# Moving the second weights, the state loads and four layer-2 steps in the opening of a fused attention and Fourier-mixing kernel

## The chip, the cores and the metric

One NeuronCore of one Trainium2 chip runs the whole program. The metric is device time in microseconds (us), the median of several executions. TensorE is written PE in the profile, VectorE DVE, ScalarE ACT, GpSimd POOL, SyncE SP. SyncE does no arithmetic here: it only issues DMAs, one after the other.

## What is computed

There are 8 batches. `x` has the shape (8 batches, 8 heads, 512 rows, 64), `state` (8, 8, 32, 64). The first part is a cross attention of x and state in both directions, per head:

```python
scores  = x @ state.T / 8 ; xread = softmax(scores) @ state      # 512 rows
scores2 = state @ x.T / 8 ; sread = softmax(scores2) @ x         #  32 rows
x = concat([xread, sread], rows)     # (8, 544, 512) after the heads are put side by side
```

The second part works on each batch's 544 x 512 matrix:

```python
mixed = real(fft(fft(x, axis=rows), axis=columns))
u  = x + mixed
un = (u - mean(u)) / sqrt(var(u) + 1e-6)          # over the 512 columns
out = u + relu(un @ w_ch1) @ w_ch2                # 512 -> 2048 -> 512
```

The real part of the two transforms is written as products with cosine and sine tables, after folding rows and columns that the tables treat alike.

## The kernel before

**Order.** The order of the work on every engine is written out by hand (a manual schedule): instructions stand on their engine in the order in which the source calls them, and each engine works strictly through its own list. What is issued behind a waiting instruction on the same engine waits with it. Batch 0 and the table set-up are the opening. Then comes one long hand-written stretch, in which batch 0's layer 1, batch 1's attention and both axes of batch 1's transform are interleaved. From there on a function `weave` mixes streams of steps for `b = 1..7` by fractions of a stage: layer 2 of batch b-1, layer 1 of batch b, the reads and the transform of batch b+1, the scores of batch b+2 and the load of x of batch b+3. A stream `(steps, lo, hi)` spreads its steps evenly between the fractions `lo` and `hi`.

**Names.**
- `load_x(b)` issues seven DMAs on SyncE (L145), which bring x of batch b into an f32 tile `xs` in packets of 256 bytes. Two `xs` tiles take turns. `cast_x` (L148) or, for batch 2, `cast_columns` (L1118) casts it on POOL into the bf16 tile `xin`.
- `turned[b]()` issues the DMA transposes on SyncE: two of the state blocks into `sT` (L377) and four of `xin` into `xT` (L388). `turned[2, 0]` is the two state transposes of batch 2 alone. `scores(i)` (PE, `esp`, L437) needs them, its results go through the exponential on ACT (L442), and `turn_scores(g)` (PE, `eTp`, L449) turns these.
- `turn_in_dram(lo, hi)` (L155) copies the states of batches lo to hi-1 from DRAM to DRAM with the 32 rows of each head in reverse order; `load_state(lo, hi, s_dram)` (L113) loads the turned states into an f32 tile; `state_blocks` (L168) writes them, as bf16, into the block-diagonal tile `stb`, four copies on POOL. The states of batches 0 to 2 lie in one tile, those of batches 3 to 7 in another.
- `first_weights(lo, hi)` and `second_weights(lo, hi)` (L310, L325) load quarters of `w_ch1` and `w_ch2` with a cast from f32 to bf16, 512 KB on the chip's side each. Their DMAs are issued by POOL, on a queue of their own.
- `gate` copies are tiny POOL instructions that read one column of a tile. Each holds POOL's list until the tile has been written: L1132 waits for w1's last quarter, L1167 for batch 2's x, L1169 for batch 1's second fold, L1172 for the last quarter of w2. The last four columns of batch 2's x are cast behind L1172, and so the transposes of batch 2's x wait for w2.
- Batch 1's reads are `r1[0]` to `r1[7]`. `r1[0]` reads the low rows and copies them on POOL (L519), `r1[1]` and `r1[2]` fold them on POOL (L523 to L531, `XEl`, `XQl`). The full rows are folded on VectorE (L534 to L549, `XQ`).
- `L[0..15]` are layer 1's steps of batch 0: 16 matmuls of 128 columns (L936) into a PSUM tile `ph`, then a Relu on ACT (L938). `M[4*i + q]` is layer 2's step of row tile i and quarter q of w2: 4 matmuls of 512 columns (L990) into the PSUM tile `po` of row tile i, which is held from q = 0 until the result is formed (`ot`, VectorE, L957) after q = 3. `ph` and `po` share three PSUM buffers (`psF`).
- `over_s1(j)` (`gp`, L783) is batch 1's transform over the rows, `over_d1(k)` (`yp`, L679 and L680) that over the columns; `add1`, `centre1` and `turn_u1` (L684, L840, L851) add, subtract the mean and turn the result for layer 1.
- `stats_of` computes mean and variance into a tile `mv` (VectorE, L339); a `root` turns it into `rstd` with two POOL instructions (L343, L344). The roots of batches 0 and 1 are collected and called late, in a block. `mv` has six buffers.
- A finished tile whose rows go out in reverse is stored to `r_dram` (L971) and from there, once that has landed, to the output (L972). Others go out directly (L961).

Of the kernel before, what the change touches and what calls it, by code (L numbers as in the profile page):

```python
# [12 lines left out]
F32 = mybir.dt.float32  # L13
# [17 lines left out]
def kernel(  # L31
# [8 lines left out]
    nc = tc.nc  # L40
    B, H, S, D = x.shape
# [11 lines left out]
    s_dram = nc.dram_tensor("s_dram", (B, H, Ns, D), F32, kind="Internal")  # L53
# [3 lines left out]
    wk = ctx.enter_context(tc.tile_pool(name="wk", bufs=2))  # L57
# [51 lines left out]
    def states(lo, hi):  # L109
        return stf[:, lo:hi] if lo < 3 else stl[:, lo - 3:hi - 3]  # L110

    def load_state(lo, hi, src=state):
        nc.sync.dma_start(  # L113
            out=states(lo, hi).rearrange("p b g d -> p (b g) d"),
            in_=src[lo:hi].rearrange("b (g hh) j d -> (hh j) (b g) d", hh=4),
        )

    xin_bufs = [singles.tile([128, 4, 514], BF16, name=f"xin{i}") for i in range(2)]
    xs_of = {}

    def load_x(b):
        xs = xs_of[b] if b in xs_of else wk.tile([128, 4 * dm], F32, name="xs", tag="xs")
        xs_of[b] = xs
        v = xs.rearrange("p (i h d) -> p i h d", i=4, d=D)
        xb = x[b].rearrange("h s d -> s h d")
        row = v[15:32:16, 3]
        parts = [
            (v[:, 0], xb[1:129]),
            (v[:, 1], xb[144:272]),
            (v[:, 2], xb[273:401]),  # L130
            (v[32:128, 3], xb[416:512]),
            (v[0:15, 3], xb[129:144]),
            (v[16:31, 3], xb[401:416]),
            (row, xb[0:273:272]),
        ]
        if b == 0:
            for queue, n in ((nc.sync, None), (nc.scalar, 2), (nc.sync, 3), (nc.scalar, 0), (nc.sync, 4), (nc.sync, 5), (nc.sync, 6),
                             (nc.sync, 1)):
                if n is None:
                    load_state(0, 1)  # L140
                else:
                    queue.dma_start(out=parts[n][0], in_=parts[n][1])
            return
        for o, rows in parts:
            nc.sync.dma_start(out=o, in_=rows)  # L145

    def cast_x(b, copy=nc.gpsimd.tensor_copy, lo=0, hi=4):
        copy(xin_bufs[b % 2][:, lo:hi, 1:513], xs_of[b].rearrange("p (i c) -> p i c", i=4)[:, lo:hi])  # L148
# [5 lines left out]
    def turn_in_dram(lo, hi):  # L154
        nc.sync.dma_start(out=s_dram[lo:hi].rearrange("b h j d -> (b h) j d"),  # L155
                          in_=state[lo:hi, :, ::-1, :].rearrange("b h j d -> (b h) j d"))
# [8 lines left out]
    def state_blocks(lo, hi, copy=nc.scalar.copy):  # L165
        for hh in range(4):
            pq = slice(32 * hh, 32 * hh + 32)
            copy(stb[pq, lo:hi, :, 4 + 64 * hh:68 + 64 * hh], states(lo, hi)[pq])  # L168
# [7 lines left out]
    gate = singles.tile([128, 4], F32, name="gate")  # L176
# [131 lines left out]
    def first_weights(lo, hi):  # L308
        for q in range(lo, hi):
            nc.gpsimd.dma_start(out=w1[:, :, q * 512:(q + 1) * 512], in_=w1v[:, :, q * 512:(q + 1) * 512])  # L310
# [12 lines left out]
    def second_weights(lo, hi):  # L323
        for q in range(lo, hi):
            nc.gpsimd.dma_start(out=w2[:, q * 4:(q + 1) * 4, :], in_=w2v[:, q * 4:(q + 1) * 4, :])  # L325
# [9 lines left out]
    def stats_of(u, name, roots=None):  # L335
        st6 = wk.tile([128, 6], F32, name="st6", tag="st6", bufs=4)
        nc.vector.bn_stats(st6, u)  # L337
        mv = wk.tile([128, 2], F32, name="mv", tag="mv", bufs=6)
        nc.vector.bn_aggr(mv, st6)  # L339
        rstd = wk.tile([128, 1], F32, name="rstd", tag=name, bufs=16)  # L340

        def root():
            nc.gpsimd.tensor_tensor(rstd, mv[:, 1:2], epst, op=ALU.add)  # L343
            nc.gpsimd.tensor_tensor(rstd, rstd, mhalf, op=ALU.pow)  # L344

        if roots is None:
            root()
        else:
            roots.append(root)
        return mv, rstd  # L350
# [347 lines left out]
    def transform(b):  # L698
# [126 lines left out]
        def spread(k, r):  # L825
            mv, rstds[k, r] = stats_of(U[k][:, r, r:r + 512], "rstd", first_roots)
# [61 lines left out]
    def low_rows(g4):  # L888
        key = ("L", g4)
        unT = wk.tile([128, DC, 128], BF16, name="unTL", tag="unTL", bufs=1)  # L890
        un_of[key] = unT
        m = {}

        def over_d():
            yp = second_axis([GLs[g4][:, c, :] for c in range(4)])
            U = m["U"] = wk.tile([128, 512], F32, name="UL", tag="UL", bufs=1)
            add_forward(U, yp, XLs[g4][:, 0:512])

        def centre():
            mv, m["rstd"] = stats_of(m["U"], "rstd")  # L900
            ub = m["ub"] = wk.tile([128, 512], BF16, name="ub", tag="ub", bufs=5)
            nc.vector.tensor_scalar(ub, in0=m["U"], scalar1=mv[:, 0:1], scalar2=None, op0=ALU.subtract)

        def turn_u():
            nc.sync.dma_start_transpose(out=unT, in_=m["ub"])
            dst = g4
            tiles_of[key] = [(m["U"], m["rstd"], dst)]

        return [over_d, centre, turn_u]
# [97 lines left out]
    def warm(n):  # L1007
        t = psF.tile([128, 512], F32, name="warm", tag="c")
        for i in range(n):
            nc.tensor.matmul(t[:, 0:128], lhsT=ident, rhs=ident, start=(i == 0), stop=(i == n - 1))  # L1010
# [56 lines left out]
    nc.gpsimd.tensor_add(ZB[0:32, 1, 0:1], XRs[0][0:32, 0, 128:129], XRs[0][0:32, 0, 384:385])  # L1067
    nc.gpsimd.memset(XB[0:32, 1, 257:258], 0.0)
    first_weights(3, 4)
    second_weights(0, 2)  # L1070
    warm(4)
    read(1)
    sread()
# [40 lines left out]
    L, M = layer1(0), layer2(0)  # L1114
    over_s1, over_d1, add1, centre1, turn_u1, done1 = transform(1)
    turns1, copies1, s1 = s1[0], s1[1:4], s1[4:]
    def cast_columns(lo, hi, i):
        nc.gpsimd.tensor_copy(xin_bufs[0][:, i, 1 + lo:1 + hi], xs_of[2].rearrange("p (i c) -> p i c", i=4)[:, i, lo:hi])  # L1118
# [12 lines left out]
    clear_state(3, B)  # L1131
    nc.gpsimd.tensor_tensor(gate, xs_of[0][:, 0:4], w1[:, :, 3 * 512], op=ALU.add)  # L1132
    load_x(2)
    turned[2, 0]()
    turn_in_dram(3, B)
    turn_u(0, 1)
    add_sums(0, 0)
    centre_sums(0, 0)
# [12 lines left out]
    L[2]()  # L1151
    s1[2]()
    r1[0]()
    r1[1]()
    r1[2]()
    L[3]()
    s1[3]()
    r1[3]()
# [5 lines left out]
    L[5]()  # L1164
    r1[6]()
    r1[7]()
    nc.gpsimd.tensor_copy(gate, xs_of[2].rearrange("p (i c) -> p i c", i=4)[:, :, 0])  # L1167
    second_weights(2, 4)
    nc.gpsimd.tensor_copy(gate, XQs[1].rearrange("p (g j c) -> p g j c", g=2, j=4)[:, 1, 3, 0:4])  # L1169
    for i in range(4):  # L1170
        cast_columns(0, 508, slice(i, i + 1))
    nc.gpsimd.tensor_copy(gate, w2[:, 12:16, 0])  # L1172
    cast_columns(508, 512, slice(0, 4))
    load_state(3, B, s_dram)
    turned[2]()
    load_x(3)
    L[6]()
    L[7]()
    turn_u(1, 0)
# [2 lines left out]
    L[8]()  # L1182
    L[9]()
    L[10]()
    over_s1(0)
    over_s1(1)
    keep_middle()
    L[11]()
    over_s1(2)
    over_s1(3)  # L1190
    M[0]()
    over_d1(0)
    add1(0, 1)
    L[12]()
# [3 lines left out]
    L[13]()  # L1198
    centre1(0, 0)
    add1(1, 1)  # L1200
    M[4]()
    turn_u1(0, 1, nc.scalar.copy)
    L[14]()
    centre1(1, 1)
    add1(1, 0)
    M[1]()
    turn_u1(0, 0, nc.scalar.copy)
    L[15]()
    centre1(1, 0)
    M[5]()  # L1210
    turn_u1(1, 1)
    M[2]()
    turn_u1(1, 0)
    spread(0, 0)
    spread(1, 1)
    spread(1, 0)
    done()
    state_blocks(3, B, nc.gpsimd.tensor_copy)
    for root in first_roots[0:1] + first_roots[5:8] + first_roots[1:5]:
        root()  # L1220
    M[6]()
    M[3]()
    done1()
    l2, scores_first = M, scores_next
    for b in range(1, B + 1):
        reads_next = reads_after
        l2, l2_now = (layer2(b), [l2[7]] + l2[8:]) if b == 1 else (layer2(b) if b < B else [], l2)
        streams = [(l2_now + (layer2(("L", b // 4)) if b in (3, 7) else []), 0, 1)]
        if b == 1:
            streams = [(l2_now[:5], 0, 0.38), (l2_now[5:], 0.6, 1)]  # L1230
        if b < B:
            streams.append((layer1(b), 0.13 if b == 2 else 0.08, 1))
        if b + 1 < B:
            if b == 1:
                streams.append((scores_first[0:2], 0, 0.08))
                streams.append((scores_first[2:4], 0.08, 0.15))
            streams.append((reads_next, 0.17 if b == 1 else 0, 0.42 if b == 1 else 0.3))
            streams.append((transform(b + 1), 0.58 if b == 1 else 0.47, 0.88 if b == 1 else 0.85))
        if b + 2 < B:
            scores_next, reads_after = attend(b + 2)  # L1240
            streams.append(([lambda: (cast_x(b + 2), turned[b + 2]())], 0.15 if b == 1 else 0.2, 0.2))
            streams.append((scores_next, 0.5, 1))
        if b + 3 < B:
            streams.append(([lambda: load_x(b + 3)], 0.35, 0.35))
        if b in (3, 7):
            streams.append((low_rows(b // 4), 0.02, 0.2))
            streams.append((layer1(("L", b // 4)), 0.36, 0.8))
        weave(*streams)
# [30 lines left out]
```

## Time and profile before

| | us |
|---|---|
| median of 5 runs | 306.15 (305.11 to 307.30) |
| the profiled execution, its time | 306.49 |
| the profiled execution, its span | 304.7 |
| PE busy / DVE / ACT / POOL in the span | 290.1 / 179.2 / 136.3 / 89.9 |
| mean granted clock of PE | 0.994 |

The profile is one execution, and times in it count from the start of its span. An instruction's busy time is its own; idle time before it is put down to what released it. `SPq` is SyncE while it issues a DMA. A DMA's time from issue to landing appears as `DMA`. "DMA share" is the mean busy share of the core's 16 DMA engines, counted by the packets' own times, so that it can pass 1.

In the profiled execution SyncE's list ran as follows: batch 2's x issued 20.94 to 34.35; two state transposes to 37.56; the turn of the states of batches 3 to 7 issued 37.61 and landed 48.03; its load issued 48.05; the transposes of batch 2's x issued 48.64 to 53.79; batch 3's x 53.84 to 58.97; the first store 59.08, its landing 61.34; a direct store to 63.30; batch 3's transposes 63.46 to 71.87; batch 4's x 72.54 to 77.67. POOL issued w2's first two quarters at 14.69 and its last two at 37.52.

### The profile page before, as it was taken

The page shows a single profiled execution, that of the slowest core. Times are in us where ns is not written, and L with a number is a line of the kernel's source. Part 1 is how long each engine was busy: PE and PEld are TensorE (multiplying, and loading weights), DVE is VectorE, ACT ScalarE, POOL GpSimd, SP SyncE. Part 2 cuts the span into 40 slices and gives each one's busy share as a digit, 9 for nine tenths or more (in the row PEclk, how much of TensorE's full clock was granted, in tenths as well). Part 3 has the DMA queues.
Part 4 walks back from the last instruction along what each step waited for, and adds up shares of the span by engine and source line. Part 5 has one row for each costly group of instructions (what it writes and reads, how often), then busy time and mean ns, then how long its engine had stood idle before and what let it go on. Part 6 is the DMA issues. An engine that isn't in the chain of part 4 may idle for free.

```text
span 304.7 us, 6022 instructions
## 1 busy us (share of the span) xinstructions
PE 290.1 (95%) x2301; PEld 165.3 (54%) x2333; DVE 179.2 (59%) x446; ACT 136.3 (45%) x253; POOL 89.9 (29%) x222
## 2 busy tenths in 40 slices
PE   5999998797999999999999999999999999999996
PEld 5789974344544555456544554445444544555443
DVE  8868985267788395764727575684668484100012
ACT  6887665335533553244433545245523442333300
POOL 6874443870272034401306022701240031000000
PEclk9999999799999999999999999999999999999999
DMA  8999596957534963457442693353343023600345
GB/s 155 206 205 202 122 151 127 189 106 160 101 87 70 180 132 104 104 127 177 87 96 59 143 180 71 84 125 69 86 90 69 37 69 86 128 12 34 71 131 145
DMA packets 110794, 34.86 MB, mean 114 GB/s; under 512 B 101950, under 2 KB 106302, under 8 KB 110766
## 3 DMA queue, kind: packets, MB, share of 16 engines
q1 hardware_dynamic: 100046, 28.72, 43.8%
q0 software_dynamic: 4224, 4.19, 8.3%
q10 hardware_dynamic: 6496, 1.57, 2.5%
q8 instruction: 18, 0.29, 0.4%
q14 instruction: 10, 0.08, 0.1%
HBM read 22.41 MB, written 14.02 MB: 120 GB/s over the span
## 4 chain that ended last, share of the span: by engine, by line
PE 74%; DMA 10%; SPq 8%; DVE 5%; issue 1%; ACT 0%; ACTq 0%
PE po L990 33%; PE ph L926 31%; DMA s_dram<-in_state_dram 6%; SPq L145 6%; PE gp L783 2%; DMA xs<-in_x_dram 2%; SPq L388 1%; PE po L982 1%; SPq L377 1%; PE yp L680 1%; PE xfp L462 1%; PE esp L437 1%; PE yp L679 1%; PE eTp L449 1%; DVE U L684 1%
## 5 line engine op out<-in xcount | busy, mean ns | idle before, releaser
L990 PE MATMUL po<-w,hT 128*128 128x512 bf16 x481 | 123.3, 381 | 1.2 <-issue 0.5
L928 ACT ACTIVATE hT<-ph 128x512 bf16<-128x512 f32 x112 | 66.9, 597 | 120.7 <-PE ph L926 118.7
L926 PE MATMUL ph<-unT,w 128*128 128x512 bf16 x431 | 113.0, 381 | 0.9 <-DMA unT<-ub 0.2
L926 PEld LDWEIGHTS <-w 128*128 128x128 bf16 x576 | 50.7, 98 | 47.5 <-issue 1.2
L990 PEld LDWEIGHTS <-hT 128*128 128x128 bf16 x496 | 46.9, 98 | 46.8 <-issue 1.1
L957 DVE SCALAR_TENSOR_TENSOR ot<-po,rstd,U 128x512 f32<-128x512 f32 (+2 forms) x33 | 24.0, 731 | 50.8 <-PE po L990 48.7
L787 POOL COPY GL<-G 128x128 bf16<-128x128 bf16 x7 | 2.0, 289 | 75.6 <-ACT G L784 75.6
L684 DVE TENSOR_TENSOR U<-yp,XR 128x512 f32<-128x512 f32 x14 | 9.5, 682 | 22.0 <-PE yp L680 22.0
L337 DVE BATCH_NORM_STATS2 st<-U 128x6 f32<-128x512 f32 x32 | 21.8, 681 | 0.1
L344 POOL TENSOR_TENSOR rstd<-rstd,mhalf 128x1 f32<-128x1 f32 x34 | 20.1, 590 | 2.7
L343 POOL TENSOR_TENSOR rstd<-mv,epst 128x1 f32<-128x1 f32 x34 | 6.6, 194 | 42.0 <-DVE mv L339 41.9
L936 PE MATMUL ph<-unT,w 128*128 128x128 bf16 x256 | 16.4, 219 | 0.3 <-DVE unT L852 0.3
L784 ACT CAST G<-gp 128x288 bf16<-128x288 f32 x28 | 13.1, 482 | 5.8 <-PE gp L783 5.6
L936 PEld LDWEIGHTS <-w 128*128 128x128 bf16 x256 | 15.1, 98 | 0.6 <-issue 0.4
L842 DVE TENSOR_SCALAR ub<-U,mv 128x512 bf16<-128x512 f32 x24 | 12.3, 513 | 0.9
L938 ACT ACTIVATE hT<-ph 128x512 bf16<-128x512 f32 x16 | 9.5, 594 | 6.1 <-PE ph L936 6.1
L148 POOL CAST xin<-xs 128x2048 bf16<-128x2048 f32 (+1 forms) x9 | 11.7, 1319 | 0.2 <-PE ph L926 0.2
L442 ACT ACTIVATE E<-esp 128x512 bf16<-128x512 f32 x14 | 8.4, 597 | 6.9 <-PE esp L437 6.9
L519 POOL COPY XT<-XR 32x514 bf16<-32x514 bf16 x7 | 4.2, 603 | 22.8 <-DVE XR L471 22.8
L471 DVE TENSOR_TENSOR XR<-xrp,rs 128x512 bf16<-128x512 f32 x14 | 9.7, 695 | 0.5
L471 DVE TENSOR_TENSOR XF<-xfp,rs 128x512 bf16<-128x512 f32 x14 | 9.7, 692 | 0.5
L684 DVE TENSOR_TENSOR U<-yp,XF 128x510 f32<-128x510 f32 x14 | 9.4, 673 | 0.0
(245 smaller groups left out, 372.0 us busy)
## 6 DMA issues: line engine op xcount, KB each, us to landing
xs<-in_x_dram SPq DMA_DIRECT2D x22, 256.0 KB, 3.3
w<-in_moe_w_ch_dram POOLq DMA_DIRECT2D x8, 512.0 KB, 9.9
out_dram<-ot SPq DMA_DIRECT2D x15, 256.0 KB, 3.4
r_dram<-ot SPq DMA_DIRECT2D x14, 256.0 KB, 2.3
out_dram<-r_dram SPq DMA_DIRECT2D x14, 256.0 KB, 3.5
xs<-in_x_dram SPq DMA_DIRECT2D x8, 192.0 KB, 4.6
xs<-in_x_dram ACTq DMA_DIRECT2D x2, 256.0 KB, 5.6
l_dram<-ot SPq DMA_DIRECT2D x2, 256.0 KB, 2.0
```

The costliest lines, as they stand in the source:

```text
L145: nc.sync.dma_start(out=o, in_=rows)
L337: nc.vector.bn_stats(st6, u)
L344: nc.gpsimd.tensor_tensor(rstd, rstd, mhalf, op=ALU.pow)
L471: nc.vector.tensor_tensor(ov, in0=p[ps, :, 0:256].rearrange("p g (h d) -> p g h d", d=D), in1=rs[ps].unsqueeze(3).to_broadcast([n, 2, 4, D ...
L684: nc.vector.tensor_add(u.rearrange("p (k r) -> p k r", r=2), p.rearrange("p (r k) -> p k r", r=2)[:, 0:u.shape[1] // 2, :], x.rearrange("p ...
L784: nc.scalar.copy(G[:, j, :].rearrange("p (i q) -> p q i", q=2), p[:, 0:NM].rearrange("p (q i) -> p q i", q=2))
L842: nc.vector.tensor_scalar(t, in0=ud, scalar1=mv[:, 0:1], scalar2=None, op0=ALU.subtract)
L926: nc.tensor.matmul(ph[:, o:o + n], lhsT=w1[:, c, f * 128:(f + 1) * 128], rhs=un_of[key][:, c, :], start=(c == 0), stop=(c == DC - 1))
L928: nc.scalar.activation(hT[:, per * i:per * i + per, :].rearrange("p a b -> p (a b)"), ph, AF.Relu, scale=-1.0 / 512 if key == 0 else -1.0 ...
L936: nc.tensor.matmul(ph[:, o:o + 128], lhsT=w1[:, c, f * 128:(f + 1) * 128], rhs=un_of[key][:, c, 128 * r:128 * r + 128], start=(c == 0), st ...
L957: nc.vector.scalar_tensor_tensor(ot[:, cols], in0=po_of[i][:, 0:cols.stop - cols.start], scalar=rstd, in1=u[:, cols], op0=ALU.mult, op1=AL ...
L990: nc.tensor.matmul(po_of[i], lhsT=h_of[key][:, f, i * 128:(i + 1) * 128], rhs=w2[:, f, :], start=(f == 0), stop=(f == FC - 1))
```

## The change

- `second_weights(0, 2)` leaves the opening. It is called behind a `gate` on batch 2's x, which moves up to just behind `r1[0]`; `second_weights(2, 4)` follows `r1[2]`. So all of w2 is issued after batch 2's x has landed, and the folds of `r1[1]` and `r1[2]` stand behind the gate on POOL.
- The states of batches 3 to 7 are split. Batch 3's is turned in DRAM right behind `load_x(2)`, loaded behind batch 2's state transposes, and copied into `stb` behind the cast of batch 2's x. Those of batches 4 to 7 are turned behind `load_x(3)`; their load and their copy become a stream of the stage b = 1, at the fractions 0.39 and 0.76.
- `mv` gets ten buffers for six.
- Of batch 0's layer 2, `M[0]` and `M[4]` move up amid `over_s1`, and `M[1]`, `M[5]`, `M[2]`, `M[6]` move up one place each; `L[11]` moves ahead of `over_s1(0)`.

```diff
-        mv = wk.tile([128, 2], F32, name="mv", tag="mv", bufs=6)
+        mv = wk.tile([128, 2], F32, name="mv", tag="mv", bufs=10)
...
     first_weights(3, 4)
-    second_weights(0, 2)
     warm(4)
...
     load_x(2)
+    turn_in_dram(3, 4)
     turned[2, 0]()
-    turn_in_dram(3, B)
+    load_state(3, 4, s_dram)
...
     r1[0]()
+    nc.gpsimd.tensor_copy(gate, xs_of[2].rearrange("p (i c) -> p i c", i=4)[:, :, 0])
+    second_weights(0, 2)
     r1[1]()
     r1[2]()
+    second_weights(2, 4)
     L[3]()
...
     r1[7]()
-    nc.gpsimd.tensor_copy(gate, xs_of[2].rearrange("p (i c) -> p i c", i=4)[:, :, 0])
-    second_weights(2, 4)
     nc.gpsimd.tensor_copy(gate, XQs[1].rearrange("p (g j c) -> p g j c", g=2, j=4)[:, 1, 3, 0:4])
     for i in range(4):
         cast_columns(0, 508, slice(i, i + 1))
+    state_blocks(3, 4, nc.gpsimd.tensor_copy)
     nc.gpsimd.tensor_copy(gate, w2[:, 12:16, 0])
     cast_columns(508, 512, slice(0, 4))
-    load_state(3, B, s_dram)
     turned[2]()
     load_x(3)
+    turn_in_dram(4, B)
...
     L[10]()
+    L[11]()
     over_s1(0)
     over_s1(1)
     keep_middle()
-    L[11]()
+    M[0]()
     over_s1(2)
     over_s1(3)
-    M[0]()
+    M[4]()
     over_d1(0)
...
     turn_u1(0, 1, nc.scalar.copy)      # M[4] stood before it, now M[1]
...
     turn_u1(0, 0, nc.scalar.copy)      # M[1] stood before it, now M[5]
...
     turn_u1(1, 1)                      # M[5] stood before it, now M[2]
     turn_u1(1, 0)                      # M[2] stood before it, now M[6]
...
     done()
-    state_blocks(3, B, nc.gpsimd.tensor_copy)
     for root in first_roots[0:1] + first_roots[5:8] + first_roots[1:5]:
         root()
-    M[6]()
     M[3]()
...
             if b == 1:
+                streams.append(([lambda: load_state(4, B, s_dram), lambda: state_blocks(4, B, nc.gpsimd.tensor_copy)], 0.2, 0.95))
```

More of the change, by code (lines that the diff above doesn't have):

```diff
@@ L1200 @@
     add1(1, 1)
-    M[4]()
+    M[1]()
     turn_u1(0, 1, nc.scalar.copy)
@@ L1205 @@
     add1(1, 0)
-    M[1]()
+    M[5]()
     turn_u1(0, 0, nc.scalar.copy)
@@ L1209 @@
     centre1(1, 0)
-    M[5]()
+    M[2]()
     turn_u1(1, 1)
-    M[2]()
+    M[6]()
     turn_u1(1, 0)
```

## The prediction

> **What bounds the kernel now.** I read the page first. TensorE is busy for 290.1 us of a span of 304.7 us, so the end moves only if one of its idle or slow stretches moves. The slices show its clock below full in one place, the eighth slice (53 to 61 us).
>
> ```profile
> PE 290.1 (95%) x2301; PEld 165.3 (54%) x2333; DVE 179.2 (59%) x446; ACT 136.3 (45%) x253; POOL 89.9 (29%) x222
> PEclk9999999799999999999999999999999999999999
> ```
>
> Next, that stretch us by us. Columns: stretch, its length, busy time of PE, PEld, DVE, ACT, POOL, granted clock, DMA share, GB/s.
>
> ```profile
> 51.00:52.00 1.00, 0.17 (x2) 0.02 (x2) 0.28 (x1) 0.00 (x0) 0.49 (x1) 1.00 0.83 154
> ...
> 54.00:55.00 1.00, 0.00 (x0) 0.00 (x0) 0.21 (x2) 0.00 (x0) 0.83 (x3) 1.00 0.46 94
> ...
> 57.00:58.00 1.00, 1.00 (x4) 0.35 (x3) 0.13 (x1) 0.42 (x3) 0.85 (x3) 0.50 1.28 227
> 58.00:59.00 1.00, 1.00 (x4) 0.41 (x3) 0.00 (x0) 0.37 (x1) 0.91 (x3) 0.50 1.36 219
> ```
>
> From 51 to 56 us TensorE idles for about 3.1 us; then it is busy at half clock. The trace's clock record has 0.50 from 56.8 to 60.2 us, which costs half of 3.4, 1.7 us. Third, the chain that ended last, in order of time: who made it idle.
>
> ```profile
> 20.94 0.39 SPq L145
> 21.38 1.40 SPq L145
> 22.84 5.46 SPq L145
> 28.34 3.43 SPq L145
> 31.81 1.37 SPq L145
> ...
> 37.61 10.42 DMA s_dram<-in_state_dram
> 48.64 1.22 SPq L388
> ...
> 52.53 2.50 DMA xT<-xin
> ```
>
> It is SyncE's queue. Issuing batch 2's x takes 13.4 us, where batch 4's takes 5.13; the turn of five states inside DRAM takes 10.42; only then come the transposes of batch 2's x. Fourth, the timelines of POOL and TensorE. A number in brackets is idle time before the instruction, and who ended it.
>
> ```profile
> 37.07 0.19 POOL L1167 COPY gate<-xs 128x4 f32<-128x4 f32 x1 [3.50 <-DMA xs<-in_x_dram]
> 37.52 1.53 POOL L325 DMA_DIRECT2D w<-in_moe_w_ch_dram  x2 [0.26 <-issue]
> 47.30 0.19 POOL L1172 CAST gate<-w 128x4 f32<-128x4 bf16 x1 [5.87 <-DMA w<-in_moe_w_ch_dram]
> ```
> ```profile
> 70.52 0.29 PE L437 MATMUL esp<-sT,xT 128*128 128x64 bf16 x4 [0.32 <-DMA xT<-xin]
> 72.71 0.24 PE L783 MATMUL gp<-TC,XQ 128*128 128x144 bf16 x1 [1.04 <-DVE XQ L543]
> ```
>
> Batch 2's x lands at 36.9 and the last of w2 at 47.2. The second fence matters later: at 70.5 TensorE is already at the heels of SyncE, for batch 3.
>
> **The change, part by part.**
>
> *w2's first two quarters leave the opening.* The trace's landings: w1's last quarter at 25.0, w2's first two at 28.4 and 31.8. Between 25 and 29 us the packets alternate one for one: some 153 of 1 KB of POOL's queue (96 ns each) and 152 of 256 B of SyncE's (30 ns) per us. So x gets a quarter of the DMA time; alone, batch 4's x moves 850 to 1030 packets per us. With w2 gone, x has the engines from 25.0 on: about 4,200 packets at 900, 4.7 us, and 0.6 to land: 30.3 instead of 36.9.
>
> *All of w2 behind x.* POOL's gate opens at 30.3; by the rows of 37.07 the issue starts 0.45 later (30.8), and by the trace its first packets flow 1.8 after that (32.6; before: 37.5 to 39.3). A quarter is 528 packets (4224 over 8) at 200 per us, 2.64 us; four are 10.6. Some 1,000 packets of 256 B (state turn, state load, sT) may alternate, at 0.03 us on one of 16 engines: 0 to 1.6 us, I take 0.8. Landing 0.3: 44.3, against 47.2. The gate and the last columns of the cast add 0.4 to 0.5: x's transposes start at 45.0 instead of 48.64, **3.6 us earlier**. Before, the turn of five states (landed 48.03) was the last of it; now one state is turned ahead, 256 rows, and hidden under w2.
>
> The Trainium skill ("SBUF — State Buffer", SBUF: two separate sides) speaks against this move: while VectorE is in a two-port mode, POOL can't write descriptors. By the rule the weights issued at 31 and 36 could stand still beside a busy VectorE, and every us of that would come off the 3.6 (at 3.6 us of it the sum is rival 3's). Measured: the issue of 37.52 fell beside VectorE at 97% and still flowed after 1.8 us.
>
> *What the gate holds up on POOL.* Behind it stand the folds of batch 1's low rows, 30.6 to 33.6 before; now they start at 32.4 and end at 35.6. VectorE takes XEl at 37.23 and TensorE XQl at 36.9 or later (L[11] now stands before, 0.9 us). Cost nothing, cover 1.5 to 2 us; past that every us of x is a us of stall.
>
> *Layer 2 steps moved.* M[0] needs w2's first quarter at about 38.4; it lands near 35.6. L[11] and M[0] fill gaps of 0.1 to 0.3 us at 36 to 40, some 0.35 us. But M[0] and M[4] now hold two of the three PSUM buffers before L[12], so L[13] waits for L[12]'s copy (ACT L938, 0.60 and its start): about 0.4 us. Zero, and M[3] still ends near 51.
>
> *Batch 2's scores.* The transposes land 2.7 to 4.9 us after their start: 47.7 to 49.9, so the scores find them. What stays is the exponential between the second scores and their turning, 0.6 to 0.8 us. The turning starts at 53.2 instead of 56.17: 2.95 us. With idle of 0.8 us the clock should stay (1.04 us of idle at 71.7 left it at 1.00): another 1.7. TensorE could be 4.65 us earlier.
>
> *Ten mean buffers.* VectorE waited 3.51 us (51.3 to 54.8) for POOL's roots, POOL for the state copy. The first results then leave at 54 instead of 55.8 to 57.1, which frees PSUM for layer 1 in time; otherwise layer 2's second step would wait up to 2 us. Needed, and within the 2.95.
>
> *SyncE up to batch 3's scores.* x3 follows the transposes: issued 50.2 to 55.3. New behind it is the turn of four states: 0.84 us of issue (the row of the larger turn), and its 1,024 packets at about 900 per us go ahead of the store to r_dram, whose landing SyncE then waits for (L972, before at 61.34). x3's packets end 3.6 us earlier, 1.1 go to the turn, 0.1 to r_dram's 2.3 us: L972 comes 2.4 to 2.8 earlier, I take 2.6. With the 8.4 us that a turn of 256 rows took beside the weights it would come later than before, but here no weights flow. Then two and four transposes (3.1 and 5.2 us), as before: the second of batch 3's lands at 67.7 instead of 70.3.
>
> *The sum.* TensorE would be at batch 3's scores at 65.3 and gets their second half at 67.9, 2.6 earlier than 70.52; it waits for SyncE some 2.3 us. The 1.04 us behind it goes, since VectorE's fold (XQ at 72.66) moves with TensorE's 4.65 and is ready at 68.0: the gain at L783 is 2.6 + 1.05 = **3.65 us**. VectorE's second fold output (L548, 74.41) would be ready at 69.8, and gp of it stands at 70.8: no bound.
>
> *Later.* load_state(4,B) costs SyncE 0.45 us in the idle 77.7 to 80.6; state_blocks costs POOL four copies of 0.6, 2.4 us, in front of two roots of batch 2 and the folds of batch 3, used over 10 us later. I put both at 0 (up to 0.5 if POOL's cover is short). From 80 us on TensorE never waits over 0.2 us, so the end moves by what L783 moves.
>
> The profiled execution took 306.49 us (span 304.7, 1.8 around it), 0.34 above the median of 306.15. 306.49 - 3.65 = 302.84, on the median's scale **302.5**.
>
> **Rivals.**
>
> 1. *The clock falls again.* The wait moves to batch 3's scores, 2.3 us with a blip. For it: half clock followed a stretch (53.4 to 56.8) in which TensorE was busy for about 1.25 of 3.4 us, and the new one can leave as little as 1.1. Against: 1.04 us did not do it. Price 1.2 to 1.7 us: 303.7 to 304.3. The Trainium skill ("TensorE: Matmul & The Clock Gate", HAM oscillation) warns of idle gaps over about 3.4 us; by that rule 2.3 would be safe and this rival void.
> 2. *SyncE isn't the bound:* w2 lands a us sooner and the turn hides. Then TensorE's own 4.65 counts: 301.5.
> 3. *SyncE takes all back:* DRAM-to-DRAM turning of four states takes 4 us on its way, or w2 lands at 46.5. The gain is then only the 1.04 of L783, less a clock loss: 305 to 306.5, no change.
> 4. *Slower: batch 2's x lands late.* POOL stands at the gate with batch 1's folds and all of w2 behind it. Landing plus 3.9 us must be below 37.7 (XQl), landing plus 14.7 below 48.64 (transposes): both turn near 34. If x still lands at 36.9, TensorE loses 3 us at 37 and the transposes come 3 later: 309. For it: from 20 to 23 us, with w1 alone in the way, SyncE's queue moved no packet. Against: 25.0 is when w1 is through.
>
> **How the numbers follow.** Forecast 0.43 (301.7 to 303.5), rival 1 0.25, rival 2 0.12, rival 3 0.12, rival 4 0.08. 0.5% of 306.15 is 1.5 us, about what a measurement of this kernel can tell from no change. Faster (below 304.6): 0.43 + 0.12 + most of rival 1 (0.16) = 0.71; the rest of rival 1 and rival 3 make 0.21; slower 0.08. Range 301.0 to 306.0: it reaches over rival 1 and into rival 3, and leaves out rival 4 and the ends of 2 and 3.
>
> **What would show it.** Right: POOL's gate on xs ends near 30.3, the gate on w2 near 44; the first L388 at about 45; no wait of esp near 51; no half clock at 57; L972 near 58.7; a wait of esp on xT of 1 to 2.5 us near 66; gp (L783) without its 1.04. Wrong: the xs gate after 34; a turn of states over 3 us after x3; a half clock after 66; a new wait for PSUM at L[13] to L[15] of over 1 us, or any wait of TensorE past 80.

## The result and the profile after

| | median (us) | runs | lowest to highest |
|---|---|---|---|
| before | 305.87 | 79 | 303.18 to 309.86 |
| after | 304.80 | 44 | 303.14 to 306.58 |

The ratio is 0.9984, with a 95% interval from 0.9969 to 0.9998. It leaves out executions more than 1.5% above the fastest of their kernel, all of them (19) of the kernel before, so the medians are further apart (1.07 us) than the ratio says (about 0.5 us). The time lies in the range given, but well above the 302.5 forecast: where a clear gain was forecast, there is next to none. The profiled execution took 305.03 us, its span 303.2, against 306.49 and 304.7.

First the page. TensorE is busy 1.5 us less, and its clock still has one dent, two slices later than before. The third line is from the list of waits (total us, times, longest).

```profile
PE 288.6 (95%) x2301; PEld 165.7 (55%) x2333; DVE 180.3 (59%) x446; ACT 136.4 (45%) x253; POOL 92.2 (30%) x226
PEclk9999999997999999999999999999999999999999
```
```profile
PE esp L437 <- DMA xT<-xin: 2.4, 2, 1.4
```

That wait stands in front of batch 3's scores. The windows around it (columns as before: PE, PEld, DVE, ACT, POOL, clock, DMA share, GB/s):

```profile
66.00:67.00 1.00, 0.22 (x2) 0.00 (x0) 0.97 (x3) 0.60 (x1) 0.00 (x0) 1.00 0.61 127
...
68.00:69.00 1.00, 0.07 (x3) 0.08 (x4) 0.97 (x4) 0.00 (x0) 0.00 (x0) 1.00 0.34 68
...
71.00:72.00 1.00, 1.00 (x4) 0.38 (x3) 0.00 (x0) 0.44 (x2) 0.00 (x0) 0.50 0.61 181
72.00:73.00 1.00, 1.00 (x8) 0.72 (x7) 0.00 (x0) 0.40 (x1) 0.00 (x0) 0.50 0.87 218
```

The stall of 51 to 56 us has become one of 66 to 69, and the half clock behind it came along: the clock record has 0.50 from 70.16 to 73.57. In the chain of waits the turn inside DRAM and batch 2's transposes are gone; what is left of SyncE there is batch 3's:

```profile
63.76 1.28 SPq L377
65.15 1.20 SPq L388
66.40 2.48 DMA xT<-xin
```

SyncE's own timeline shows each step of the sum (start, length, what):

```profile
46.17 5.12 SPq L388 DMA_TRANSPOSE xT<-xin  x4
51.33 5.09 SPq L145 DMA_DIRECT2D xs<-in_x_dram  x7
56.46 0.62 SPq L155 DMA_DIRECT2D s_dram<-in_state_dram  x1
57.19 0.59 SPq L971 DMA_DIRECT2D r_dram<-ot  x1
60.49 0.64 SPq L972 DMA_DIRECT2D out_dram<-r_dram  x1
65.15 5.12 SPq L388 DMA_TRANSPOSE xT<-xin  x4
```

Batch 2's transposes start at 46.17 (48.64 before, 45.0 forecast), L972 at 60.49 (61.34 before, 58.7 forecast). Of 2.5 us won at the top of the list 0.85 are left at L972. POOL's and TensorE's timelines give the two ends:

```profile
30.66 0.19 POOL L1154 COPY gate<-xs 128x4 f32<-128x4 f32 x1 [1.39 <-DMA xs<-in_x_dram]
31.12 1.53 POOL L325 DMA_DIRECT2D w<-in_moe_w_ch_dram  x2 [0.27 <-issue]
34.49 0.90 POOL L528 TENSOR_TENSOR XQl<-XEl 32x128 bf16<-32x128 f32 x1
...
45.80 0.19 POOL L1174 CAST gate<-w 128x4 f32<-128x4 bf16 x1 [2.29 <-DMA w<-in_moe_w_ch_dram]
```
```profile
67.60 0.29 PE L437 MATMUL esp<-sT,xT 128*128 128x64 bf16 x4 [1.38 <-DMA xT<-xin]
68.93 0.29 PE L437 MATMUL esp<-sT,xT 128*128 128x64 bf16 x4 [1.03 <-DMA xT<-xin]
69.92 0.23 PE L783 MATMUL gp<-TC,XQ 128*128 128x144 bf16 x1
```

Batch 2's x is there at 30.66, as forecast; w2 lands 14.7 us after its issue instead of 13.5. The second half of batch 3's scores runs at 68.93 instead of 70.52, and L783 without a wait at 69.92 instead of 72.71, 2.8 us earlier. From L783 to the end of the span it takes 233.3 us instead of 232.0: the half clock now falls behind L783, before it fell ahead of it. 2.8 less 1.3 is the 1.5 us by which the two profiled executions differ.

**One profile is not the kernel.** An execution's mean granted clock tells how many stretches of half clock it had: in the profiled ones 0.999 or 1.000 goes with none, 0.993 or 0.994 with one of 3.4 us, 0.988 with two. Sorted so, all executions of the two kernels whose clock is on record (number, median us; below 0.991 counts as two, from 0.997 on as none):

| | no stretch | one | two |
|---|---|---|---|
| before, four chips, 107 | 19, 304.1 to 305.0 | 35, 306.2 to 306.5 | 53, 307.8 to 308.8 |
| after, 68 | 29, 303.9 to 304.9 | 38, 305.4 to 306.1 | 1, 308.3 |

(The medians are those of the single chips.) With as many stretches on the same chip the changed kernel is only 0.1 to 0.55 us faster: 303.94 against 304.19 and 305.69 against 306.23 on one chip, 304.85 against 304.97 and 306.08 against 306.53 on another. The rest of the difference of the medians is that two stretches, half of all executions before, hardly occur any more.

### The profile page after: what moved, and what is told of

It is laid out like the page before. It is cut to its first block, busy times and chain, and to the rows that moved or that the text cites. A ratio compares the mean times of both kernels' runs of the same rounds, so it can differ in the third digit from the quotient of the medians.

```text
span 303.2 us, 6027 instructions
## 1 busy us (share of the span) xinstructions
PE 288.6 (95%) x2301; PEld 165.7 (55%) x2333; DVE 180.3 (59%) x446; ACT 136.4 (45%) x253; POOL 92.2 (30%) x226
## 4 chain that ended last, share of the span: by engine, by line
PE 84%; DVE 8%; ACT 2%; DMA 2%; issue 2%; SPq 1%; POOL 0%; DVEq 0%; POOLq 0%
PE po L990 35%; PE ph L926 32%; PE ph L936 3%; PE gp L783 3%; PE yp L680 1%; PE esp L437 1%; PE po L982 1%; PE yp L679 1%; PE xfp L462 1%; PE xrp L462 1%; DVE U L684 1%; DMA xT<-xin 1%; DVE st L337 1%; PE eTp L449 1%; DMA unT<-ub 1%
## 5 line engine op out<-in xcount | busy, mean ns | idle before, releaser
L926 PEld LDWEIGHTS <-w 128*128 128x128 bf16 x576 | 50.9, 98 | 47.3 <-issue 1.1
L784 ACT CAST G<-gp 128x288 bf16<-128x288 f32 x28 | 12.9, 483 | 6.6 <-PE gp L783 6.4
```

Of the source, the lines that this page charges most:

```text
L784: nc.scalar.copy(G[:, j, :].rearrange("p (i q) -> p q i", q=2), p[:, 0:NM].rearrange("p (q i) -> p q i", q=2))
L926: nc.tensor.matmul(ph[:, o:o + n], lhsT=w1[:, c, f * 128:(f + 1) * 128], rhs=un_of[key][:, c, :], start=(c == 0), stop=(c == DC - 1))
```

## The experiments

The theory after the result: SyncE's list from batch 2's transposes to batch 3's still sets the pace; what w2 gave at its top the turn of four states takes back at its bottom, and the wait it leaves costs clock. Rivals: the front (folds held up behind the gate) takes the gain; the clock alone does it; w2's move brings nothing in the first place. The table collects the times of SyncE's list in the profiled executions, against the forecast's: POOL's gates on batch 2's x and on w2, the first transposes of batch 2's x (S2), L972, the second half of batch 3's scores, L783.

| | x2 gate | w2 gate | S2 | L972 | scores | L783 | half clock from |
|---|---|---|---|---|---|---|---|
| forecast | 30.3 | 44.3 | 45.0 | 58.7 | 67.9 | 69.06 | none |
| before | 37.07 | 47.30 | 48.64 | 61.34 | 70.52 | 72.71 | 56.8 |
| before again (e15) | 36.95 | 47.23 | 48.60 | 61.48 | 69.89 | 71.00 | none |
| after | 30.66 | 45.80 | 46.17 | 60.49 | 68.93 | 69.92 | 70.2 |
| after again (e5) | 30.80 | 46.41 | 46.77 | 60.87 | 69.23 | 70.22 | none |
| after again (e9) | 32.15 | 47.59 | 47.95 | 62.43 | 71.01 | 72.90 | 70.2 (6.8 us) |
| weights only (e6) | 30.70 | 48.24 | 48.61 | 61.30 | 70.51 | 72.68 | 56.4 |
| states only (e7) | 36.77 | 46.14 | 46.50 | 60.67 | 69.11 | 70.10 | none |
| states, late turn (e8) | 37.19 | 46.45 | 46.82 | 59.54 | 67.93 | 69.19 | none |
| after, late turn (e10) | 30.96 | 46.61 | 46.98 | 59.86 | 68.30 | 69.34 | none |

### The turn of four states, later (e1_turn_late, e10_turn_late_again)

```diff
     load_x(3)
-    turn_in_dram(4, B)
...
             if b == 1:
+                streams.append(([lambda: turn_in_dram(4, B)], 0.2, 0.3))
```

> The changed kernel, with the turn of the states of batches 4 to 7 moved from between batch 3's x and the first store to behind batch 3's transposes. Theory (SyncE's list up to batch 3's scores sets the time, and the half clock behind the wait takes the rest): the first store's landing comes 0.7 us (issue) plus 1 to 2 us (the turn's packets) earlier, the wait of esp for xT falls from 2.4 us to under 1 us, the half clock at 70 us goes, and the time falls by 2 to 3.5 us against the changed kernel, to 301.5 to 303. Rival (the front of the stage, where VectorE's and POOL's folds run slower side by side, sets the time): no change within 0.5 us.

> The changed kernel with the turn of batches 4 to 7 behind batch 3's transposes, beside the changed kernel on one chip. Theory (the turn delays SyncE's list by 1.5 us up to batch 3's scores, which are the bound): 1 to 1.5 us faster than the changed kernel within the executions without a half clock, and fewer with one: median 302.7 to 303.3. Rival (something else binds at 70 us): the same as the changed kernel.

e1 took 303.88 us beside 307.69 for the kernel before (0.9876, 0.9839 to 0.9913); e10, on another chip, 303.53 (0.9878, 0.9832 to 0.9923) beside 305.84 for the changed kernel itself (e9). So moving one DMA down SyncE's list is worth 2.3 us on that chip, 1.3 of it among the executions without a half clock (304.85 against 303.53). e10's list:

```profile
46.98 5.12 SPq L388 DMA_TRANSPOSE xT<-xin  x4
52.14 5.38 SPq L145 DMA_DIRECT2D xs<-in_x_dram  x7
57.63 0.36 SPq L971 DMA_DIRECT2D r_dram<-ot  x1
59.86 0.69 SPq L972 DMA_DIRECT2D out_dram<-r_dram  x1
...
69.70 0.61 SPq L155 DMA_DIRECT2D s_dram<-in_state_dram  x1
```

From S2 to L972 it takes 12.9 us here, 12.7 and 12.9 in the kernel before, 14.1 to 14.5 in the changed one: the turn costs 1.5 us where it stood. 0.7 is its issue, 0.8 to 1.1 the later landing of the store behind it (L971 to L972: 3.30 after, 2.26 before, 2.23 here). TensorE waits 1.3 us at batch 3's scores instead of 2.4 to 3.0, and none of the 12 executions had a half clock. In e1, where w2 came late (gate at 47.89), TensorE also waited for w2 at `M[0]`, 1.29 us; that step's cover is thin.

### Matmuls in the wait (e2_fill, e11_fill_again)

```diff
+    def dummies(n):
+        t = qt("dummy")
+        for i in range(n):
+            nc.tensor.matmul(t[:, 0:128], lhsT=ident, rhs=ident, start=True, stop=True)
...
             if b == 1:
+                scores_next[0] = lambda s=scores_next[0]: (dummies(45), s())
```

> The changed kernel, with 45 extra matmuls of 128 columns (about 2.5 us at full clock, results unused) ahead of batch 3's first scores, where TensorE waits 2.4 us for SyncE's transposes. Theory (the half clock follows from that idle stretch and costs about 1.5 us in the executions that have it): the clock stays at 1.00 in all executions and the median falls by 0.7 to 1.3 us against the changed kernel; the end of the wait itself (esp at 68.9) does not move. Rival (the clock falls for another reason, or its loss is made up behind it): the half clock stays, or the median does not fall.

> The changed kernel with 45 extra matmuls ahead of batch 3's first scores, beside the changed kernel on one chip. Theory (the half clock comes from the idle stretch in front of these scores): no execution with a half clock, all at the level of the changed kernel's undisturbed ones, so the median falls by the share of half-clock executions times 1.5 us (0.5 to 0.9). Rival: half clocks stay, or the extra matmuls cost as much as they save.

The changed kernel with 45 matmuls of nothing in front of batch 3's scores. e11: 304.91 us, beside 305.84 for the changed kernel (e9), which is that kernel's time without a half clock on this chip (304.85). e2: 305.40 (0.9924, 0.9893 to 0.9954). None of the 20 executions had a half clock. So the idle time causes it, and it costs about 0.9 us of the median. Windows of e9 and, in the second fence, e11:

```profile
68.00:69.00 1.00, 0.00 (x0) 0.00 (x0) 1.00 (x2) 0.33 (x1) 0.00 (x0) 1.00 0.55 114
...
74.00:75.00 1.00, 1.00 (x4) 0.32 (x3) 0.00 (x0) 0.59 (x2) 0.00 (x0) 0.50 0.74 195
```
```profile
68.00:69.00 1.00, 1.00 (x22) 1.00 (x19) 0.96 (x3) 0.00 (x0) 0.00 (x0) 1.00 0.32 65
```

The traces also show why the same wait costs clock in one execution and not in the next. The clock changes only at the ends of windows of 3.413 us (clock windows below): the stretches at full clock in the record last for example 47.79, 61.44, 232.11 and 296.96 us, all whole multiples of it, and the windows between can be counted off from there. 17 profiles have such a record. From 10 to 290 us the clock fell once in each of six (before, after, e3, e6, e9, e13), every time behind a clock window in which TensorE was busy for 0.80 to 1.52 us. Every other clock window at full clock has 1.59 us or more (the 1.59 is e7's), and the clock stayed. The changed kernel's wait in its first profile and, in the second fence, in e5, where it was as long (2.4 us):

```profile
66.75:70.16 3.41, 1.52 (x16) 0.94 (x17) 3.28 (x10) 0.74 (x3) 0.00 (x0) 1.00 0.45 92
```
```profile
64.09:67.50 3.41, 2.41 (x13) 0.97 (x10) 3.07 (x6) 1.79 (x3) 0.56 (x2) 1.00 0.45 107
67.50:70.91 3.41, 1.97 (x21) 1.29 (x22) 3.28 (x10) 1.09 (x2) 0.00 (x0) 1.00 0.47 96
```

In the first one clock window holds nearly the whole wait, in e5 two share it. Where they lie differs from one execution to the next.

### Folds before the gate (e3_folds_first)

```diff
-    nc.gpsimd.tensor_copy(gate, xs_of[2]...)
-    second_weights(0, 2)
     r1[1]()
     r1[2]()
-    second_weights(2, 4)
+    nc.gpsimd.tensor_copy(gate, xs_of[2]...)
+    second_weights(0, 4)
```

> The changed kernel, with POOL's folds of batch 1's low rows ahead of the gate on batch 2's x, and all four quarters of w2 issued together behind it. Theory (POOL's folds and VectorE's folds slow each other when they run at the same time; SyncE sets the end): POOL's folds take 0.45 instead of 0.9 us each, VectorE's SS 0.69 instead of 1.06, gp (L783) starts about 1 us earlier; w2 lands within 0.7 us of 45.8; the time moves by under 0.7 us, since SyncE's list is not earlier. Rival (the front sets the time): 1 us faster than the changed kernel, about 303.8.

306.93 us (0.9985, 0.9945 to 1.0025): no gain. It tells something of the front all the same. In the changed kernel POOL's folds fall beside VectorE's, and both get slower; here they are done before. VectorE's line L539 and POOL's L528, first e3, whose rows the changed kernel's follow:

```profile
33.96 0.70 DVE L539 TENSOR_TENSOR SS<-Sm 128x514 f32<-128x514 bf16 x1
```
```profile
31.36 0.45 POOL L528 TENSOR_TENSOR XQl<-XEl 32x128 bf16<-32x128 f32 x1
```
```profile
34.02 1.06 DVE L539 TENSOR_TENSOR SS<-Sm 128x514 f32<-128x514 bf16 x1
```

VectorE's last fold (L549) starts at 39.4 in the changed kernel, at 38.2 here, and the 1.2 us lead to nothing at L783 later (72.90): SyncE decides there. w2, issued in one go at 33.09, opened its gate at 47.80, 14.7 us later as well, so S2 came at 48.17 and TensorE waited 2.8 us at batch 3's scores. Since w2 starts 2 us later here, the run can't tell what the earlier folds alone would be worth.

### Matmuls in the wait of the kernel before (e4_before_fill)

```diff
+                for i, n in ((0, 14), (1, 26), (2, 10)):
+                    scores_first[i] = lambda s=scores_first[i], n=n: (dummies(n), s())
```

> The kernel before, with 50 extra matmuls of 128 columns (14, 26 and 10; results unused) ahead of batch 2's two scores steps and the turning of them, in the stretch of 51 to 56 us in which TensorE idles 3.1 us. Theory (the half clock behind that stretch costs 1.7 us in the executions that have it, and it is the same loss as behind the new wait of the changed kernel): the clock stays at 1.00 and the median falls by 0.8 to 1.7 us, to about the changed kernel's time. Rival (the idle, not the clock, is what the kernel before loses): no faster than before.

306.90 us (0.9995, 0.9953 to 1.0037). The half clocks became fewer (9 executions without, 3 with one, none with two; before on this chip 3, 7, 15), but those without took 306.3 us, 2.2 more than the kernel before without (304.1): here the matmuls themselves stand in the way. So the clock of the kernel before is a matter of its idle time too, but what it costs can't be read from this run.

### The changed kernel again (e5_after, e9_after_again)

> The changed kernel once more, on one chip with the next three. Its profile and clocks are a second sample: if the new list of SyncE sets the time, the start of the transposes of batch 2's x (46.2 us in the first profile) moves with the landing of batch 2's x, 15.5 us behind it, and the second scores of batch 3 follow 22.7 us after that start. Executions with a half clock should be slower by 1.2 to 1.7 us than those without.

> The changed kernel, as the base for the next three on the same chip. Expected 304 to 304.8 us, in two groups: about 304.0 without a half clock and 305.5 with one.

No edit. e5: 304.21 us (0.9965, 0.9928 to 1.0002); e9, on another chip, 305.84 (0.9946, 0.9911 to 0.9981). The table shows how much the list moves from one execution to another: batch 2's x lands at 30.7 in the one and 32.0 in the other, and with it S2 (46.77 and 47.95). In e9's profile TensorE waits 2.00 and 1.03 us at batch 3's scores, and the half clock lasts from 70.15 to 76.98, twice as long.

### The two halves alone (e6_weights_only, e7_states_only)

e6 has only the hunks of the opening, `r1[0]` to `r1[2]` and the gate; e7 only those of the states. On the kernel before:

```diff
# e6
-    second_weights(0, 2)               # in the opening
...
     r1[0]()
+    nc.gpsimd.tensor_copy(gate, xs_of[2]...)
+    second_weights(0, 2)
     r1[1]()
     r1[2]()
+    second_weights(2, 4)
# e7
+    turn_in_dram(3, 4)
     turned[2, 0]()
-    turn_in_dram(3, B)
+    load_state(3, 4, s_dram)
...
     load_x(3)
+    turn_in_dram(4, B)
...
+                streams.append(([lambda: load_state(4, B, s_dram), lambda: state_blocks(4, B, nc.gpsimd.tensor_copy)], 0.2, 0.95))
```

> The kernel before with the weights' move alone (all of w2 behind batch 2's x). Theory (w2 takes some 14.7 us from its issue behind x to its landing, so this move alone gives the transposes of batch 2's x little: they start at 46 to 48.3, before 48.2 to 48.6): 0 to 2 us faster than the kernel before. Rival, the prediction's own sum (45.0): 3 us faster or more, since no turn stands behind batch 3's x.

> The kernel before with the split of the states alone. Theory (w2's last two quarters no longer share the engines with a turn of five states, and land 8 to 8.5 us after an issue at 37.0; batch 3's small turn is hidden): the transposes of batch 2's x start at 45.5 to 46.5, as early as in the changed kernel or earlier, the store's landing gives 1.5 us back to the turn of four states, and the time is that of the changed kernel or below. Rival (the weights' move is what brings the changed kernel its gain): the transposes start at 47.5 or later, the time is that of the kernel before.

e6: 305.83 us (1.0005, 0.997 to 1.004), e7: 306.01 (1.0002, 0.9968 to 1.0036). Neither gains. SyncE's lines of the two:

```profile
31.13 0.84 SPq L155 DMA_DIRECT2D s_dram<-in_state_dram  x1
42.69 0.41 SPq L113 DMA_DIRECT2D gen<-s_dram  x1
48.61 5.15 SPq L388 DMA_TRANSPOSE xT<-xin  x4
```
```profile
46.50 5.12 SPq L388 DMA_TRANSPOSE xT<-xin  x4
...
60.67 0.64 SPq L972 DMA_DIRECT2D out_dram<-r_dram  x1
```

In e6 x lands 6 us earlier, and S2 not at all: w2 now takes 17 us from issue to gate, beside a turn of five states that takes 11.6 (its issue to the load behind it). In e7 w2's first half is in the opening as before, and S2 starts at 46.50 all the same. So the earlier S2 comes from the states that no longer run beside the weights, and w2's move adds nothing to it: in the three profiles with the split and without that move (e7, e8, e12) S2 lies at 46.50 to 46.82, with it (after, e5, e9, e13, e14) at 46.17 to 47.95. e7 keeps the turn of four states behind batch 3's x and has its L972 14.2 us behind S2.

The forecast that e7 would be as fast as the changed kernel failed all the same: 306.01 against 304.21 us on this chip (e5). Among executions with the same number of half clocks the difference is 0.4 to 0.6 us; the rest is that ten of e7's 12 had one, of e5's five. Whether that is chance or comes from what e7 lacks (w2's move, the mean buffers, the layer-2 steps), no run shows.

### States split, turn late, weights where they were (e8_states_turn_late)

e7 with ten mean buffers and the late turn of e1.

> The split of the states alone, with ten mean buffers, and the turn of batches 4 to 7 behind batch 3's transposes instead of between batch 3's x and the first store. Theory (SyncE's list sets the time up to batch 3's scores): transposes of batch 2's x at 45.5 to 46.5, those of batch 3's 1.5 us earlier than in the run with the split alone, the wait of esp for xT under 1.5 us, no half clock, 301.5 to 303. Rival (the front of the stage or the clock sets it): no faster than the split alone.

303.31 us (0.9944, 0.991 to 0.9978) beside 306.01 for e7 and 304.21 for the changed kernel (e5). L972 is 12.7 us behind S2. Ten of 12 executions had no half clock, the others one. So the split and the late turn bring this gain without w2's move. (e8 also has ten mean buffers; e13 below shows no use of them.) Whether w2's move adds something to it is open, since e8 and e10 ran on different chips.

### The held-back store after the own one (e12_store_swap, e16_late_swap_steps)

```diff
-            while later:
-                later.pop()()
+            due = later[:]
+            later.clear()
...
+            for go in due:
+                go()
```

> The run with split states, ten mean buffers and late turn, and in addition each second half of a store by way of r_dram issued behind the next store instead of ahead of it, so that SyncE does not stand at the landing of r_dram before batch 3's transposes. Theory (SyncE's list up to batch 3's scores is the bound): those transposes come 1 to 1.2 us earlier (from 64.2 to about 63), the wait of esp for xT falls under 0.6 us, no half clock, 302 to 302.5. Rival (TensorE's own work or VectorE's fold binds by then, or the later landing of outputs costs at the end): no faster than without it, 303.1 to 303.3.

> The changed kernel with the late turn, the second halves of the stores behind the next store, and layer 2's steps at the places of before: a try for a faster version. Theory: no half clock, 302.5 to 303.3 us. Rival: the same as with the late turn alone (303.5), since TensorE's front and VectorE's fold bind by then.

On e8: 303.60 us (0.9876, 0.9831 to 0.9922), no faster than e10 on the same chip. The own store (L961) is now issued while SyncE would wait for the landing that L972 needs, batch 3's transposes start at 63.79 instead of 64.16 (e8), the scores run at 67.60, and now VectorE's fold is late:

```profile
69.11 0.24 PE L783 MATMUL gp<-TC,XQ 128*128 128x144 bf16 x1 [0.36 <-DVE XQ L543]
```

With w2's move in addition and the layer 2 steps at their old places (e16): 304.06 (0.9902, 0.9864 to 0.994). None of these 13 executions had a half clock. So VectorE is next: L783 comes only 0.1 us earlier than in e8 and 0.2 earlier than in e10.

### Mean buffers and steps (e13_mv6, e14_steps_back)

```diff
# e13: the changed kernel
-        mv = wk.tile([128, 2], F32, name="mv", tag="mv", bufs=10)
+        mv = wk.tile([128, 2], F32, name="mv", tag="mv", bufs=6)
# e14: the changed kernel, L[11], M[0], M[4], M[1], M[5], M[2], M[6] at their old places
-    L[11]()
     over_s1(0)
...
-    M[0]()
+    L[11]()
...
```

> The changed kernel with six mean buffers again. Prediction's step: VectorE then waits for POOL's roots and frees the PSUM of the first two results later, so that layer 2's second step waits up to 2 us. Theory now: SyncE binds at batch 3's scores with 2 to 3 us to spare in front of them, so this wait costs under 0.5 us in the executions without a half clock, and may even fill the wait. Rival: up to 2 us slower than the changed kernel.

> The changed kernel with layer 2's steps and L[11] at the places that they had before. Theory (the front has 2 to 3 us to spare up to batch 3's scores): within 0.4 us of the changed kernel in each clock group. Rival (filling the gaps at 36 to 40 us brings time, or the moved steps' waits for w2 and PSUM cost it): over 0.5 us one way or the other.

e13: 306.07 us (0.9981, 0.9947 to 1.0014), 304.83 without (4 executions), 306.27 with one half clock (6) and 307.85 with two (2); e14: 305.65 (0.9951, 0.9924 to 0.9977), 304.72 and 305.96. The changed kernel did not run on this chip; on e9's it has 304.85 and 306.08, and with one half clock the kernel before takes the same on both (306.47 and 306.53). Both groups of both runs lie within 0.2 us of that. In e13's profile VectorE waits for no root of POOL between 45 and 60 us: with the state copies behind those roots gone, six buffers suffice.

### The kernel before again (e15_before_again)

> The kernel before, for a second profile of it. Theory: its executions fall into groups by the number of half-clock stretches (none, one, two of 3.4 us), at about 304.2, 306.3 and 308.2 us; a profile with two shows the second one right behind batch 3's scores or joined to the first. Without the turn of four states in its list, the store's landing comes 12.7 us behind the start of batch 2's transposes, against 14.3 in the changed kernel.

Two executions, 304.41 and 309.78 us. The profiled one had the same stall and no half clock behind it (windows, then TensorE's timeline):

```profile
54.00:55.00 1.00, 0.00 (x0) 0.00 (x0) 0.14 (x2) 0.00 (x0) 0.84 (x3) 1.00 0.41 85
...
57.00:58.00 1.00, 1.00 (x7) 0.41 (x6) 0.21 (x1) 0.74 (x3) 0.92 (x4) 1.00 1.27 214
```
```profile
55.02 0.41 PE L437 MATMUL esp<-sT,xT 128*128 128x64 bf16 x8 [1.38 <-DMA xT<-xin]
...
69.89 0.29 PE L437 MATMUL esp<-sT,xT 128*128 128x64 bf16 x4 [1.00 <-DMA xT<-xin]
```

So the half clock is drawn anew in each execution. Without it the kernel before already reaches the second half of the scores at 69.89 and L783 at 71.00, only 0.8 us after the changed kernel's 70.22 (e5).

## Why the prediction was wrong

- **What binds, right.** SyncE's list up to batch 3's scores sets L783, and TensorE comes ahead of it: it waits 2.4 us there (2.3 forecast), and the stall at 51 to 56 is gone (0.6 us is left, 0.6 to 0.8 forecast).
- **x2, right in the mechanism, up to 2 us late.** 30.66, 30.80 and 32.15 against 30.3. Rival 4's point of 34 was not reached.
- **w2, mis-sized.** The sum had 2.64 us a quarter and 0.8 for alternation, 11.4. (Its own terms give a start of the transposes at 44.7 to 44.8; it wrote 45.0.) By the packet records of the changed kernel it flowed from 32.6 to 45.3, 12.7 us. In full flow it moves the 200 packets per us of the sum, but each issue starts slowly, 29 and 116 in its first two us, and 119 again at 39 behind the second one. The second start alone doesn't explain it: in e3, issued in one go, w2 flowed for 12.8 us too. What the Trainium skill ("SBUF — State Buffer", SBUF: two separate sides) would let one fear, descriptors that stand still beside VectorE, was not seen as a standstill: the first packet went 1.5 us after the issue, as early as the sum had it. Where the slow start behind an issue comes from, no run shows. In the five profiles with the changed kernel's list (after, e5, e9, e13, e14) S2 lies at 46.2 to 47.95, 47.3 on average, against 48.6: 1.3 to 1.4 us instead of **3.6**.
- **The turn of four states, mis-sized.** 1.5 us instead of 1.0. The sum counted its packets; the queue pays its issue, and then the later landing of the store as well. The two misses together make the failed step: L972 lies at 60.5 to 62.4, 61.6 on average over those five profiles, against 61.3 and 61.5. The **2.6 us** of the sum at that place are zero, except in the profiled pair, where 0.85 is left.
- **The half clock, rival 1 with too small a chance and a wrong zero.** It came back in 39 of 68 executions, not in 1 of 4, at 1.2 to 1.8 us each. And the forecast took the 1.7 us of the profile of before as that kernel's own. They are one draw of none, one or two; of the 2.8 us that L783 won in the profiled pair, 1.7 is the difference between the two profiles of the kernel before (72.71 with a half clock, 71.00 in e15 without). In e15 the wait of 1.04 at L783 isn't there at all, so the sum's 1.05 for it was part of the draw too. Nor did the 1.04 us of idle that left the clock at 1.00 speak for the new wait: by the rows shown with e11 it is the work inside one clock window that tells (1.34 us in the kernel before's, which rival 1 read as about 1.25), not the longest idle piece.
- **w2's move, wrong.** All of the 3.6 us was put down to it together with the split of the states. e6 and e7 show that the split alone gives S2 its gain. The run with the split alone still did not beat the kernel before in time.
- **Ten mean buffers, wrong; steps and front, right.** "Needed" is disproved by e13. The moved steps cost and bring nothing (e14), and nothing shows a part of POOL's late folds in the time (e3), though for another reason than the sum's: the front does come later, by a us (TensorE at batch 3's scores at 66.2 instead of 65.3), and the wait for SyncE covers it.
- **Later, right.** From L783 to the end it takes 231.9 us in e5 and 231.6 in e15, both without a half clock.

Rival 3 came nearest: it had w2 at 46.5 and a time unchanged. Two small slips carry nothing: from 51 to 56 us TensorE idles 2.9 us by the windows, not 3.1, and rival 1's upper end is 302.5 + 1.7 = 304.2. Open stays where the second stretch of the kernel before lies: no profile caught it. e9's lies right behind the first, after a clock window at half clock in which TensorE was busy for 2.56 us; in the other five the clock came back after 3.0 us or more.

Of the versions run those with the late turn are the fastest. The changed kernel with it takes 303.53 us, 0.9878 of the kernel before, and is 2.3 us ahead of the changed kernel on the same chip; e12, on that chip too, has 303.60, and e8, on another, 303.31. These runs can't rank the three. Most of what they win over the kernel before is its half clocks: without one, the kernel before is only 1.0 to 1.5 us behind them on their chips, and 0.2 behind e1.

## What to carry to other kernels

A queue in order pays for every entry up to the instruction that is waited for: what is taken away at its top is worth nothing if another entry goes in further down, so move that one past the waited-for entry, and add up issue and landing. Where the clock falls behind a stall, take several executions of the kernel before, sorted by granted clock, before its loss is booked as a gain: the stall is the kernel's, the loss is drawn. And when two moves feed one start, try each alone: one of them may do nothing for it.

## What the runs showed of the hardware

- A wait of 2.4 us with 0.3 of work in it was enough for a half clock of 3.41 us, and 3.0 us in e9 for 6.83; in e7 and e14 waits of 2.6 and 2.8 us cost none. In these profiles it fell behind a clock window of 3.413 us with at most 1.52 us of busy TensorE, and never behind one with 1.59 or more. 38 of 68 executions of the same program had one stretch and 29 none. The Trainium skill ("TensorE: Matmul & The Clock Gate", HAM oscillation) gives gaps over about 3.4 us as the condition; here shorter ones did it, in some executions, depending on how much of the wait one clock window holds.
- Folds on POOL and VectorE side by side slow each other: POOL's three took 0.90 us each instead of 0.45, VectorE's L539 1.06 instead of 0.70. It agrees with the Trainium skill ("SBUF — State Buffer", Who interferes with whom): a VectorE instruction with two SBUF inputs contends with a GpSimd one that reads SBUF.
- A turn inside DRAM beside the weights slows them: w2 took 17 us from issue to gate beside the turn of five states (11.6 us, e6), 14.7 in the changed kernel. The turn of four states behind batch 3's x, where no weights flow, delayed SyncE's list by 1.5; its own length no run shows.
